# A planned operation order for a gated linear-attention block: a planner that holds GpSimd's small operations back behind VectorE's two-operand operations

## The chip, the cores and the metric

The kernel runs on 1 core of one Trainium2 chip. It is one launch that reads its inputs from HBM and writes its output there. The metric is device microseconds of one execution; lower is better. Before the change the median of three runs is 526.1 us (525.42 to 526.38).

## The reference

The input x has 2048 rows (tokens) of 512 values, all fp32. After a layer norm two branches start from the same normalized rows, and their product is added to x:

```python
x = A_x
xn = _layernorm(x, axis=-1)
s = _A_ref(xn, A_wqkv, A_wo)                        # linear attention
g = _silu(_B_ref(xn, B_w1, B_w2, B_w3, B_w4))       # shift mixer and MLP
return x + s * g
```

The attention has 32 heads of 16 values. With phi(t) = t+1 for t > 0, else exp(t), it forms per head the matrix kv = sum over tokens of phi(k) v and the vector z = sum of phi(k), and for each token o = phi(q) kv / phi(q) z; o is multiplied by wo. It isn't causal, so kv needs all tokens before any o can be made.

```python
h = _gelu(_layernorm(x, axis=-1) @ w1)
# the four 128-column groups of h are shifted by +1, -1, +2, -2 tokens
hs = jnp.concatenate([g0, g1, g2, g3], axis=-1) @ w2
x1 = x + hs
h2 = _gelu(_layernorm(x1, axis=-1) @ w3) @ w4       # 512 -> 1376 -> 512
return x1 + h2
```

## The kernel before, in words

**Tiling.** There are 16 row tiles of 128 tokens, in 4 blocks of 4 tiles (512 tokens). The rows come twice: as they are (x) and with columns on the partitions (xt). Matmuls in fp32 are split: an operand a is rounded to a shorter form, ah (usually on ScalarE, `rounded`, line 451 on), and the rest al = a - ah is made on VectorE (`split`, line 460). A product is three matmuls, ah bh, al bh, ah bl. So names end in h and l. A few matmuls with a column of sums (wqm, w1m, zp) or small weights (kv, m) are done in full fp32, in two passes.

**Stages.** In the first part each tile i gets k (`key`, line 727), q (`query`, 740) and four matmul groups into g (`gram`, 750: the sum of k times x over tokens, in the four accumulators acc); per block, h (`mix1`, 794) and the w2 product by a seven-product scheme on halves (`mix2` and `seven`, 850 and 757; banks pbm, pam, pem). Then from g the matrices kv and m are made, and the second part does w3 and w4 for each block (`up_last`, `up_pair`, `down`; banks pb, pa, pe and acc) and the attention output s (`attend`, `attend_pair`). `gate` (1118) joins both and stores.

**What each tile needs from the small operations.** `moments` (575) takes mean and variance of a tile on VectorE (BN_STATS, BN_AGGREGATE, into mv). `scale_x` (585) makes from them, on GpSimd, w (variance plus eps), rs (its power -1/2, `power`, line 580), ns = -rs and nm = mean times ns, for one, two or three tiles at once. ScalarE uses rs, ns and nm as scales for the relu and exp of k and q (kr, kt, qr, qe) and for x itself. `scale_u` (596) makes pu and au, from which `spread_a` and `join_a` (603, 612) make a row of factors (ab on TensorE, ar on ScalarE, a store to and a load from DRAM: abc) by which h is multiplied (ht). `split_halo` (640) copies the two edge tokens on either side of a block into u_h and u_l, 16 operations of two values per partition on GpSimd for each block. `mixed` (866) makes the second norm's factors rs2 and nm2 per block and the normalized y, which VectorE transposes.

**GpSimd also issues DMAs** that add into their target (`gather`, 217): the sum over phi(k) into zacc, qe onto qr in DRAM (pqd), x onto o, and the three that add the chunks of w1 into w1t (`center`, 554). The next of these waits until the one before has landed. What stands behind such a waiting DMA on GpSimd's queue waits too.

**What sets the order.** No engine order is written by hand. `Plan.add` (96) records each operation with its engine, a planned duration and what it reads and writes. `deadlines` (238) gives every operation a due time, from the nominal time of the TensorE operation that needs it back through its producers (`backward`, 259: a producer is due before its consumer by its latency, a DMA by 4 us and 4 us per MB); an operation that reads PSUM is due at the latest PATIENCE after it can start. `nudged` (232) moves single due times sooner, by 0.25 us times the number in the table SOONER (operation number, number). `emit` (265) then runs a list schedule: for each engine it computes for each ready operation the earliest start, from the engine, the inputs, the buffer slots and, for operations marked `two` (VectorE or GpSimd with large operands in SBUF, line 169 on), the variable `port`; among those that could start within `slack` of the earliest it takes the one with the earliest due time, and emits it. On TensorE, an operation later in the program may go first if it lies within `window` us; `lead` bounds how long before its due time a tile is allocated. The planned times decide only the order in which operations stand on each engine's queue (SP's and GpSimd's queues among them). On the chip each queue runs in that order, and an operation starts as soon as its own semaphores allow.

**Buffers.** counts (424): 89 SBUF pieces of 512 columns, 4 PSUM banks "mm" and 4 "acc". The four h products of a block fill the four mm banks, so the next k needs a bank that ht has freed.

Of the kernel before, what the change touches and what calls it, by code (L numbers as in the profile page):

```python
# [85 lines left out]
class Plan:  # L86
# [6 lines left out]
    def new(self, tag, name, dtype=F32, width=512, rows=P):  # L93
        return Tile(self, tag, name, dtype, width, rows)

    def add(self, eng, busy, lat, reads, writes, emit, two=False, table=None, mb=0.0):
        op = Op()
        op.eng, op.busy, op.lat, op.emit, op.two, op.table, op.mb = eng, busy, lat, emit, two, table, mb
        op.pre, op.post, op.tiles, op.opens = {}, [], {}, False
        op.order = len(self.ops)  # L100
# [56 lines left out]
    def act(self, out, src, func, scale=1.0, bias=None):  # L157
        nc = self.nc
        psum = out.tile.psum or src.tile.psum
        lat = .17 + out.n / 1200 + (.09 if isinstance(scale, View) else 0) + (0 if psum else .02)  # L160
        table = 0 if func == AF.Exp else 1 if func in (AF.Gelu_apprx_tanh, AF.Tanh) else None

        def emit():
            kw = {} if bias is None else {"bias": bias.get()}
            nc.scalar.activation(out.get(), src.get(), func, scale=get(scale), **kw)  # L165

        self.add("ACT", lat - .1, lat, [src, scale, bias], [out], emit, table=table)
# [55 lines left out]


    GAP = .06
    PATIENCE = 3.0
    COLD, COLD_TILL = 1.84, 5.8
    SAFE = 2.0
    early = 0.0
# [8 lines left out]
    def deadlines(self, first):  # L238
# [8 lines left out]
        for op in self.ops:  # L247
# [3 lines left out]
            elif any(t.psum for t in op.tiles):  # L251
                op.due = min(op.due, op.at + self.PATIENCE)
            elif op.soon:
# [5 lines left out]
    def backward(self):  # L259
        for op in reversed(self.ops):  # L260
            if op.eng != "PE":
                for o in op.post:
                    op.due = min(op.due, o.due - self.GAP - (4.0 + op.mb * 4 if op.mb else op.lat))

    def emit(self, first, lead, reserve, window, ahead, table=()):
        self.deadlines(first)
# [10 lines left out]
        free = {e: 0.0 for e in avail}  # L277
        slots = {tag: [(0.0, i) for i in range(n)] for tag, n in self.counts.items()}
        port, dma = 0.0, 0.8
        under = [0.0] * 8, [0.0] * 8  # L280
        table = 0
        done = set()
# [2 lines left out]
        while left:  # L285
# [5 lines left out]
            for e, cands in avail.items():  # L291
                picks = []
                low = INF
                for op in cands:
                    s = max(free[e], op.ready)
                    if op.mb:
                        s = max(s, under[e == "POOL"][0] + self.GAP)
                    if op.two and s < port:
                        s = port
                    if op.table is not None and op.table != table:  # L300
                        s = max(s, free[e] + 1.28)
                    ok = True
                    fresh = [t for t in op.tiles if t.ap is None]
                    for t in fresh:
                        if t.tag not in slots:
                            continue
                        q = slots[t.tag]
                        need = sum(1 for u in fresh if u.tag == t.tag)
                        if len(q) < need:
                            ok = False  # L310
                            break
                        s = max(s, q[need - 1][0] + self.GAP)
                        if e == "PE":
                            if op is not front and (len(q) < 2 or op.nom - front.nom > ahead):
                                ok = False
                                break
                        elif t.tag in lead:
                            n = lead[t.tag] * (1.5 if len(q) > reserve[t.tag] else 1)
                            s = max(s, op.due + slip - n - t.early)
                    if not ok:  # L320
                        continue
                    if e == "PE" and op.nom - front.nom > window:
                        continue
                    q = s
                    if op.table is not None and op.table != table and op.due + slip < s:
                        q = s - 1.28
                    picks.append((q, s, op))
                    low = min(low, q)
                if not picks:
                    continue  # L330
                slack = .02 if e == "PE" else 0.15
                s, op = min(((s, op) for q, s, op in picks if q <= low + slack), key=lambda x: (x[1].due, x[1].order))
                if best is None or s < best[0]:
                    best = (s, op)
            if best is None:
                raise RuntimeError("no operation can go: " + str({t: len(q) for t, q in slots.items()}))
            s, op = best
            e = op.eng
# [19 lines left out]
                under[soft].append(op.end)  # L358
            if op.two:
                port = op.end if e == "POOL" else free[e]  # L360
            if op.table is not None:
                table = op.table
            for t in op.tiles:
# [23 lines left out]
def linear_attn_gated_by_mixer(  # L387
# [43 lines left out]
    pl = Plan(nc, pools, counts, ("acc", "mm"))  # L431
# [813 lines left out]
    b = NQ - 1  # L1245
# [43 lines left out]
    for b in range(NQ):  # L1289
# [50 lines left out]
        else:  # L1340
# [17 lines left out]
                gate(b * QT + QT - 1, a, o, D // 2, late=True, by_dma=False, whole=o > 0)  # L1358

    SOONER = (  # L1360
# [6 lines left out]
    )  # L1367
    pl.emit(first=6.0, lead={"p": 10.0, "w": 10.0, "ab": 10.0}, reserve={"p": 8, "w": 1, "ab": 0}, window=7.0,
            ahead=6.0, table=SOONER)


# [35 lines left out]
```

## Time and profile before

| | before |
|---|---|
| runs, us | 526.38, 526.1, 525.42; median 526.1 |
| profiled execution, us | 525.5 |
| its span, us | 523.3 |
| granted TensorE clock, mean | 0.997 |
| HBM read and written, MB | 60.33 and 30.81 |
| mean DMA rate, GB/s | 191 |

The span goes from the first to the last instruction of the profiled execution; the execution's own time is 2.2 us longer. Engines: PE is TensorE (PEld its weight loads), DVE VectorE, ACT ScalarE, POOL GpSimd, SP the queue that issues most DMAs. A timeline row gives start, duration, engine, line of the kernel, operation, output <- inputs by the program's names (buffer and tile numbers left out), form and count, and in brackets the idle time of that engine just before it, with what ended it. Matmuls are pipelined and their ends are modelled, so two rows overlap; the distance between starts is the safer measure. In a windows row stand the window, its length, the busy time and instructions of PE, PEld, DVE, ACT and POOL, the granted clock, the DMA share and GB/s.

### The profile page before, as it was taken

The numbers are of one execution on the slowest core, as the hardware profiler recorded it, in microseconds if no ns is written. First come the engines' busy times: TensorE is split into PE (matmuls) and PEld (weight loads), VectorE is DVE, ScalarE is ACT, GpSimd is POOL, SyncE is SP. The second block draws the span as 40 slices with busy tenths as digits, with TensorE's granted clock in tenths as the row PEclk, the third lists the DMA queues.
The fourth block names the chain that finished last, engine by engine and source line by source line (L and its number), as shares of the span: only waits on it lengthen the run. The fifth ranks groups of instructions, "written<-read, shape, count | busy, mean of one in ns | idle before, by whom it ended". The sixth has DMA issues, their size and how long they took to land.

```text
span 523.3 us, 8899 instructions
## 1 busy us (share of the span) xinstructions
PE 514.9 (98%) x3027; PEld 448.5 (86%) x3027; DVE 374.3 (72%) x743; ACT 319.4 (61%) x649; POOL 112.1 (21%) x207
## 2 busy tenths in 40 slices
PE   8999999999999999999999999999999999999996
PEld 7777788888888888898899889899899898999985
DVE  5949885658474837999997557897667678396735
ACT  4678995587458847958756655546463366543721
POOL 3374612721273023211200022000040000310000
PEclk9999999999999999999999999999999999999998
DMA  8957849763984369999585759838489376994904
GB/s 240 335 116 180 157 123 235 154 164 94 188 214 142 69 132 200 262 275 307 198 283 176 244 144 220 279 114 231 108 166 314 126 228 129 213 263 153 352 4 121
DMA packets 73713, 100.13 MB, mean 191 GB/s; under 512 B 7892, under 2 KB 31716, under 8 KB 73668
## 3 DMA queue, kind: packets, MB, share of 16 engines
q1 hardware_dynamic: 62436, 79.24, 47.5%
q0 software_dynamic: 11088, 20.19, 23.7%
q8 instruction: 24, 0.39, 0.3%
q14 instruction: 21, 0.17, 0.1%
q10 hardware_dynamic: 144, 0.13, 0.1%
HBM read 60.33 MB, written 30.81 MB: 174 GB/s over the span
## 4 chain that ended last, share of the span: by engine, by line
PE 82%; ACT 6%; DMA 5%; POOL 2%; DVE 2%; issue 1%; SPq 0%; ACTq 0%; POOLq 0%
PE acc L146 22%; PE pb L146 10%; PE h L146 6%; PE g L146 6%; PE q L146 5%; PE pe L146 5%; PE k L146 5%; PE pbm L146 4%; PE pbs L146 3%; DMA w1t<-in_w 3%; PE pa L146 2%; PE a L146 2%; PE pem L146 2%; PE pes L146 2%; PE s L146 2%
## 5 line engine op out<-in xcount | busy, mean ns | idle before, releaser
L221 POOL DMA_DIRECT2D xo<-x1d x12 | 10.7, 1124 | 166.0 <-ACT xo L165 165.9
L221 POOL DMA_DIRECT2D zacc<-kr x16 | 14.4, 899 | 79.1 <-DVE kr L197 71.9
L221 POOL DMA_DIRECT2D th<-in_x x14 | 12.1, 888 | 71.1 <-issue 47.9
L165 ACT ACTIVATE p<-pb 128x256 f32<-128x256 f32 x20 | 7.6, 381 | 30.6 <-PE pb L146 30.3
L197 DVE SCALAR_TENSOR_TENSOR kr<-kt,kr 128x512 f32<-128x512 f32 x16 | 11.1, 691 | 17.0 <-ACT kt L165 17.0
L221 POOL DMA_DIRECT2D o<-x x16 | 15.2, 948 | 34.6 <-DVE o L187 26.1
L165 ACT ACTIVATE gf<-gf 128x512 f32<-128x512 f32 (+1 forms) x40 | 20.9, 523 | 0.9
L197 DVE SCALAR_TENSOR_TENSOR kt<-wneg,mv,k 128x512 f32<-128x512 f32 x16 | 11.9, 743 | 10.9 <-PE k L146 10.8
L165 ACT ACTIVATE x<-x,nm,rs 128x512 f32<-128x512 f32 x16 | 12.1, 806 | 10.5 <-POOL nm L187 10.5
L221 POOL DMA_DIRECT2D pqd<-qe x16 | 17.3, 1079 | 4.6 <-ACT qe L165 3.9
L165 ACT ACTIVATE th<-xo 128x512 f32<-128x512 f32 (+1 forms) x16 | 9.7, 614 | 13.0 <-DVE xo L187 12.1
L165 ACT ACTIVATE p<-pe 128x256 f32<-128x256 f32 x20 | 7.7, 384 | 16.3 <-PE pe L146 16.3
L187 DVE TENSOR_TENSOR gf<-pa,p 128x256 f32<-128x256 f32 x20 | 8.5, 423 | 11.0 <-ACT p L165 5.4
L577 DVE BATCH_NORM_STATS2 st<-o 128x6 f32<-128x512 f32 x16 | 10.9, 686 | 6.5 <-DMA o<-x 6.0
L165 ACT ACTIVATE kr<-kt,rs 128x512 f32<-128x512 f32 x16 | 11.5, 718 | 5.5 <-POOL rs L583 4.2
L187 DVE TENSOR_TENSOR gf<-u,pe 128x256 f32<-128x256 f32 x20 | 8.3, 417 | 7.8 <-PE pe L146 7.8
L165 ACT ACTIVATE qe<-q,ns 128x512 f32<-128x512 f32 x16 | 10.8, 676 | 4.0 <-PE q L146 3.8
L197 DVE SCALAR_TENSOR_TENSOR qz<-pq,zb 128x512 f32<-128x512 f32 x16 | 10.8, 684 | 2.3 <-PE acc L146 2.3
L165 ACT ACTIVATE y<-o,nm,rs 128x512 f32<-128x512 f32 x16 | 11.9, 802 | 0.6 <-POOL nm L192 0.6
L187 DVE TENSOR_TENSOR f_10l<-gf,f_10h 96x512 fp32r<-96x512 f32 x4 | 2.7, 679 | 13.2 <-ACT gf L165 7.5
L192 POOL TENSOR_SCALAR w<-mv 128x4 f32<-128x4 f32 (+3 forms) x11 | 5.5, 498 | 30.9 <-DVE mv L578 30.6
L165 ACT ACTIVATE ht<-ht 128x512 f32<-128x512 f32 x16 | 9.5, 624 | 4.1 <-DVE ht L187 4.0
(1567 smaller groups left out, 2203.2 us busy)
## 6 DMA issues: line engine op xcount, KB each, us to landing
w_s<-in_w SPq DMA_DIRECT2D x28, 256.0 KB, 4.9
x<-in_x SPq DMA_DIRECT2D x16, 256.0 KB, 5.4
zacc<-kr POOLq DMA_DIRECT2D x16, 256.0 KB, 3.4
pqd<-qr SPq DMA_DIRECT2D x16, 256.0 KB, 2.6
pqd<-qe POOLq DMA_DIRECT2D x16, 256.0 KB, 5.0
o<-x POOLq DMA_DIRECT2D x16, 256.0 KB, 4.6
x1d<-o SPq DMA_DIRECT2D x16, 256.0 KB, 4.5
pq<-pqd SPq DMA_DIRECT2D x16, 256.0 KB, 4.7
```

The lines of the kernel that those rows point to most:

```text
L146: lambda: nc.tensor.matmul(out.get(), lhs.get(), rhs.get(), start=start, stop=stop, skip_group_check=more))
L165: nc.scalar.activation(out.get(), src.get(), func, scale=get(scale), **kw)
L187: self.vec(eng, out, [a, b], lambda: self.e(eng).tensor_tensor(out.get(), a.get(), b.get(), op=op), True)
L192: lambda: self.e(eng).tensor_scalar(out.get(), a.get(), get(s1), get(s2), **kw), False,
L197: lambda: self.nc.vector.scalar_tensor_tensor(out.get(), a.get(), get(s), b.get(), op0=op0, op1=op1),
L221: lambda: self.nc.gpsimd.dma_start(out.get(), get(src), accum_op=ALU.add), mb=mb)
L577: pl.add("DVE", .62, .69, [xv], [st], lambda: nc.vector.bn_stats(st.get(), xv.get()))
```

## The change

The same operations are emitted, in another order. The planner's `emit` gets a list, lock, of the last eight planned stretches in which VectorE runs an operation marked `two`; the planned start of a GpSimd operation that is neither a DMA nor marked `two` is moved to 0.02 us after such a stretch when it would fall into it. No wait is added to the program for it. Constants of the planner change with it: an operation that reads PSUM may wait 5 us instead of 3, a DMA is due 1 us earlier, the slack of the choice on all engines but TensorE is 0.4 us instead of 0.15, window is 12 us instead of 7, the lead of tiles "w" 20 us instead of 10; and the table SOONER is another one.

```diff
     GAP = .06
-    PATIENCE = 3.0
+    PATIENCE = 5.0
...
-                    op.due = min(op.due, o.due - self.GAP - (4.0 + op.mb * 4 if op.mb else op.lat))
+                    op.due = min(op.due, o.due - self.GAP - (5.0 + op.mb * 4 if op.mb else op.lat))
...
         port, dma = 0.0, 0.8
+        lock = [(-1.0, -1.0)] * 8
...
                     if op.two and s < port:
                         s = port
+                    if e == "POOL" and not op.mb and not op.two:
+                        s = next((b + .02 for a, b in lock if a <= s < b), s)
...
-                slack = .02 if e == "PE" else 0.15
+                slack = .02 if e == "PE" else 0.4
...
                 port = op.end if e == "POOL" else free[e]
+            if op.two and e == "DVE":
+                lock = lock[1:] + [(s, free[e])]
...
     SOONER = (
-        23, 920, 25, 567, 27, 1578, 32, 434, 33, 142, 37, 71, 40, 69, 41, 8, 43, 71, 47, 73, 49, 1817, 51, 1534,
...
+        23, 795, 26, 123, 28, 878, 29, 115, 31, 67, 32, 4, 34, 76, 35, 9, 37, 23, 38, 8, 41, 19, 44, 14, 47, 13,
...
     )
-    pl.emit(first=6.0, lead={"p": 10.0, "w": 10.0, "ab": 10.0}, reserve={"p": 8, "w": 1, "ab": 0}, window=7.0,
+    pl.emit(first=6.0, lead={"p": 10.0, "w": 20.0, "ab": 10.0}, reserve={"p": 8, "w": 1, "ab": 0}, window=12.0,
             ahead=6.0, table=SOONER)
```

What this does to the queues, from the changed program's instruction order (most differences lie in the first 80 us and from 223 to 262 us of the profile before):

| engine | before | after |
|---|---|---|
| VectorE, start | u_0h, wk_0h, wk_0l, u_0l | u_0h, u_0l, wk_0h, wk_0l |
| TensorE, start | ksum of chunks 0 and 1, then k0 and k1 of chunk 1 | ksum of chunk 0; those of 1, 2 and 3 (h) after chunk 1's k0 and k1 |
| GpSimd | w1t DMA ahead of tile 1's w, rs, ns, nm | behind them |
| GpSimd | second w1t DMA, four halo operations, w, rs, ns, nm of tiles 2 and 3 | second w1t DMA, w, rs, ns, nm of tiles 2 and 3 |
| GpSimd | first pqd DMA, then w, pu, au of block 1 | w, pu, au, then the first pqd DMA |
| SP | loads of w2 among and behind the stores pqd | loads of w1 first, then xt, x and w2, all ahead of the first pqd store |
| TensorE | q3, w1m, gram of tile 3, k4 | q3, gram of tile 3, k4, w1m |
| VectorE | w_s x4, moments of tiles 4, 5, 7, w_0l ... | moments of tiles 4 to 7, two w2 forms, kt4, w_s x4, w_0l ... |
| VectorE | w_t4l, ht0 x4 | ht of group 0, w_t4l, the other three ht |
| TensorE, 245 to 260 us | s0 and s1 (24 matmuls each) spread among the pb, pe products | s0 and s1 behind them, with single acc matmuls between them |
| ScalarE, 250 to 257 us | y12, y13, p1, y14, y15, p5 | y12, y13, y14, a weight copy, y15, p1, two copies, p5 |
| VectorE, 245 to 250 us | m_b and gf operations, then the moments of tiles 13 and 15 | moments first, then m_b and gf |

10 rows, old and new, of the table SOONER are left out of this document.

## The prediction

> **What bounds the kernel now.** I read the page first (busy time and the chain of waits), then TensorE's own timeline row by row, and then, for each hole in it, the timelines of the engines that end it.
>
> ```profile
> span 523.3 us, 8899 instructions
> PE 514.9 (98%) x3027; PEld 448.5 (86%) x3027; DVE 374.3 (72%) x743; ACT 319.4 (61%) x649; POOL 112.1 (21%) x207
> PE 82%; ACT 6%; DMA 5%; POOL 2%; DVE 2%; issue 1%; SPq 0%; ACTq 0%; POOLq 0%
> ```
>
> TensorE is busy for 514.9 of 523.3 us and holds 82% of the chain, so an order of the same operations can win only what TensorE waits. How long it waits is the distance between two matmul starts, less the step at which matmuls follow each other. The chain gives that step: twelve 512-wide matmuls in 2.77 us (0.23 us each), six 256-wide ones in 0.71 us (0.12 us each).
>
> ```profile
> 101.40 2.77 PE k L146 x12
> ...
> 499.95 0.71 PE pes L146 x6
> ```
>
> ```profile
> 34.44 0.50 PE L146 MATMUL g<-k2h,x2h 128*128 128x512 f32 x1
> 35.16 0.50 PE L146 MATMUL g<-k2l,x2h 128*128 128x512 f32 x1 [0.23 <-DVE k2l L197]
> ...
> 40.61 1.02 PE L146 MATMUL w1m<-w1t,ones 128*128 128x512 f32 x2
> ...
> 49.92 0.40 PE L146 MATMUL q<-wq_3h,u_3l 128*128 128x512 f32 x1
> 50.70 0.27 PE L151 MATMUL ab<-ident,au 128*4 128x128 f32 x1 [0.39 <-POOL au L583]
> ...
> 61.72 0.39 PE L146 MATMUL h<-u_3h,w_3l 128*128 128x512 f32 x1
> 62.43 0.51 PE L146 MATMUL k<-wk_0h,u_0h 128*128 128x512 f32 x1 [0.32 <-DVE ht L187]
> ...
> 75.73 0.28 PE L146 MATMUL pem<-w_t1h,hs10l 128*128 128x256 f32 x1
> 76.41 0.39 PE L146 MATMUL pbm<-w_t2h,hs20h 128*128 128x256 f32 x1 [0.40 <-ACT p1m L165]
> ...
> 256.27 0.28 PE L146 MATMUL s<-m_b11h,q1h 128*128 128x256 f32 x1
> 257.14 0.38 PE L146 MATMUL pe<-yb220h,w_s1h 128*128 128x256 f32 x1 [0.59 <-ACT p L165]
> ```
>
> Start to start, less the step, the holes are 35.16-34.44-0.23 = 0.49; 50.70-49.92-0.23 = 0.55; 62.43-61.72-0.23 = 0.48; 75.73 to 76.41 less 0.12 = 0.56; 256.27 to 257.14 less 0.12 = 0.75. The matmul after a hole takes about 0.1 more (its weights were not loaded ahead), and 0.27 more goes just before 34.44. Together: some 3.6 us, all in the first 80 us but one. After 260 us there is no hole worth naming. So the gain has a ceiling near 3.6 us; the loss has none.
>
> **The change, part by part.** It adds and removes no operation: every engine has the same instructions in another order. What counts is what stands ahead of the instruction that ended each hole, in the changed program's order. I go from the start to the end.
>
> First the reason for holding small operations back. The same operation (two values per partition) takes 0.73 us while VectorE works without a gap and 0.20 us when it has stopped:
>
> ```profile
> 28.03 0.73 POOL L648 TENSOR_TENSOR u_0l<-hal,u_0h 128x2 fp32r<-128x2 f32 x1
> ...
> 29.44 0.20 POOL L648 TENSOR_TENSOR u_1l<-hal,u_1h 128x2 fp32r<-128x2 f32 x1
> ```
>
> The planner's start times are no waits, though; a queue starts an operation when its inputs are there. Only places in the queue change.
>
> Start, +0.35 us. VectorE now makes u_0l second, ahead of its half of wk_0h and of wk_0l:
>
> ```profile
> 5.12 0.29 DVE L192 TENSOR_SCALAR u_0h<-xt 128x256 fp32r<-128x256 f32 x1 [5.12 <-DMA xt<-in_xt]
> 5.33 0.28 DVE L192 TENSOR_SCALAR wk_0h<-wk_s 128x256 fp32r<-128x256 f32 x1
> 5.73 0.69 DVE L187 TENSOR_TENSOR wk_0l<-wk_s,wk_0h 128x512 fp32r<-128x512 f32 x1
> 6.34 0.42 DVE L187 TENSOR_TENSOR u_0l<-xt,u_0h 128x256 fp32r<-128x256 f32 x1
> ```
>
> TensorE waits for both wk_0 pieces; they come up to 0.42 later, and the short wait for u_0l goes. Bounds 0 and +0.45. The sum over wk (ksum) now ends before k0 and k1 do, so kt of block 0 starts about as early as VectorE's list did; k0l and x1l stay ahead of their matmuls by some 0.2 us. I take nothing for that stretch.
>
> Hole at 34.4 us, -0.87 (0.27+0.49+0.1). It goes back through kr of tile 2 to GpSimd:
>
> ```profile
> 18.04 1.09 POOL L221 DMA_DIRECT2D w1t<-in_w  x1 [5.75 <-DMA w1t<-in_w]
> ...
> 27.34 0.95 POOL L221 DMA_DIRECT2D w1t<-in_w  x1 [1.39 <-DMA w1t<-in_w]
> ...
> 29.85 0.23 POOL L192 TENSOR_SCALAR w<-mv 128x2 f32<-128x2 f32 x1
> ```
>
> ```profile
> 10.08 0.74 POOL L192 TENSOR_SCALAR w<-mv 128x1 f32<-128x1 f32 x1 [7.01 <-DVE mv L578]
> ...
> 12.10 0.19 POOL L187 TENSOR_TENSOR nm<-mv,ns 128x1 f32<-128x1 f32 x1
> ```
>
> ```profile
> 16.27 0.68 DVE L577 BATCH_NORM_STATS2 st<-x 128x6 f32<-128x512 f32 x1
> ```
>
> The second w1t gather waits until the first has landed, and everything on GpSimd queues behind it. Then came halo operations from 28.03 on, and only at 29.85 the statistics of tiles 2 and 3. In the new order these stand directly behind the gather: 28.03 instead of 29.85, 1.8 us sooner. Against that, the first gather now stands behind the four operations of tile 1's statistics (for tile 0 from 10.08 to 12.29, 2.2 us), and tile 1's moments take about the place that tile 2's had on VectorE, 16.27 to 16.95: the gather starts near 19.1, 1 us later. Left are 0.85 us, and TensorE itself comes 0.35 later: together more than the hole. Bounds -0.87 and +0.15 (first rival).
>
> The gather took 9 us to land. The Trainium skill (DMA: Bandwidth & Descriptors, section Queues, rings and completion order) says that each DMA engine takes turns packet by packet between the queues that have work. By that it would land in far less than 9 us beside the loads, also after a later start, and the next term would be zero; the trace (18.04 to 27.05) shows no such turn, and I go by the trace.
>
> Third gram (tile 3), +0.35. w1m moves from ahead of it to behind k4, so TensorE is there at 40.61+0.35-0.87 = 40.1. ScalarE needs 9.42 us from kr of tile 2 to k3h, and VectorE 1.43 from k3h's start to k3l's end:
>
> ```profile
> 30.92 0.72 ACT L165 ACTIVATE kr<-kt,rs 128x512 f32<-128x512 f32 x1 [3.44 <-POOL rs L583]
> ...
> 40.34 0.71 ACT L165 ACTIVATE k3h<-kr,tiny 128x512 fp32r<-128x512 f32 x1
> ```
>
> With kr at 30.1, k3l ends near 40.9, and its matmul wants it at 40.3: 0.6, less up to 0.3 of ScalarE waits that the new order of x3, kr3, kt3 takes out. Bounds -0.1 and +0.8.
>
> Hole at 50 us, -0.55. The last au waited because the moments of its three tiles stood behind w1's centering on VectorE and ended late:
>
> ```profile
> 46.49 1.87 DVE L577 BATCH_NORM_STATS2 st<-x 128x6 f32<-128x512 f32 x3
> ...
> 48.50 0.66 DVE L187 TENSOR_TENSOR w_0l<-w_s,w_0h 128x512 fp32r<-128x512 f32 x1
> ```
>
> ```profile
> 49.60 1.04 POOL L583 TENSOR_TENSOR au<-pu,nhalf 128x4 f32<-128x4 f32 x1
> ```
>
> Now these moments stand ahead of the centering, and au ahead of the first pqd gather, so it is ready before q4 is through. In exchange the centering starts only after k4: from w1m's end VectorE needs four w_s operations and w_0l, 0.6 each (the three moments above go at 0.62), so about 3.1, and TensorE has 12 x 0.23 of q4, two small transposes and two matmuls of h, about 3.4. That cover is thin: without it, up to 0.3. Bounds -0.55 and 0. The loads of w2 that VectorE now uses ahead of the centering stand on SP's queue ahead of the first pqd store, which waits for qr; so they come before that wait and hold nothing up.
>
> Hole at 62 us, -0.59 (0.48+0.11). k5 needs a PSUM bank, and the first ht, which frees one, stood behind the whole of w2's splitting:
>
> ```profile
> 61.69 2.48 DVE L187 TENSOR_TENSOR ht<-h,abc 128x512 f32<-128x512 f32 x4
> ```
>
> In the new order ht0 goes before w_t4l and fewer w2 operations stand ahead of it, so it has a start of at least one operation (0.6), and more as VectorE runs earlier. Bounds -0.59 and 0.
>
> Hole at 76 us, -0.5. p1m could not be copied before the second table load and two exponentials:
>
> ```profile
> 72.58 1.28 ACT L165 ACT_TABLE_LOAD   x1
> ...
> 75.99 0.36 ACT L165 ACTIVATE p1m<-pbm 128x256 f32<-128x256 f32 x1
> ```
>
> With ht early, gelu and all that follows move ahead by up to 2 us (the last ht waits for h3 on TensorE), TensorE by some 1.3; I count most of 0.67. Bounds -0.67 and 0.
>
> Hole at 256 us, -0.85 (0.75+0.1). Two y copies that waited for GpSimd's nm stood ahead of p5:
>
> ```profile
> 249.61 1.50 POOL L192 TENSOR_SCALAR w<-mv 128x4 f32<-128x4 f32 x1 [10.57 <-DVE mv L578]
> ...
> 253.03 0.55 POOL L192 TENSOR_SCALAR nm<-nm 128x4 f32<-128x4 f32 x1
> ```
>
> ```profile
> 253.62 1.53 ACT L165 ACTIVATE y<-o,nm,rs 128x512 f32<-128x512 f32 x2 [0.57 <-POOL nm L192]
> ```
>
> Now the last moments stand ten VectorE operations sooner (six of about 0.6, four shorter), and I take 2.7 us of it, since other operations moved ahead of them as well. nm is then there at 253.58-2.7 = 250.9 (times of before). But all four y copies (0.75 each) and a weight copy stand ahead of p1: p1 starts at 250.9+3.0+0.6 = 254.5, before TensorE needs it at 255.46. Bounds -0.85 and +3.7 (second rival: 1.9, and 1.8 gained ahead that is lost).
>
> New waits, +0.65. With s0 moved back, only three 0.23 matmuls lie between the third and fourth product in one bank, where 12 lay, and the gf addition between them comes behind an m_b split: 0.25. And VectorE has no room there:
>
> ```profile
> 240.00:260.00 20.00, 19.41 (x151) 18.61 (x150) 18.62 (x39) 16.53 (x38) 3.72 (x4) 1.00 0.71 235
> ```
>
> (TensorE, weight loads, VectorE 18.62 of 20, ScalarE.) For holes that I can't see I add 0.4, somewhat less than one of the size of those above; bounds of the two together 0 and +1.5.
>
> Sum: +0.35-0.87+0.35-0.55-0.59-0.5-0.85+0.65 = -2.0. The profiled execution took 525.5 us (its span is 523.3), so 523.5; the three runs' median, 526.1, is 0.6 above it, so the runs should show 524.1.
>
> **The rivals.** First, less gain: the first gather lands late. It speaks for it that VectorE has no gap from 13 us until its k1l and x1l are done after 29 us, and that the gather landed slowly in just that stretch. The Trainium skill (SBUF — State Buffer, section Who interferes with whom) says that descriptor writing by GpSimd is starved while VectorE holds the shared port in a two-port mode. If the landing waits for VectorE's stretch, which ends about 0.4 later than 29.3, the second gather goes at 29.9 instead of 28.3, kr of tile 2 comes at 31.7 or somewhat before, and the hole at 34.4 grows to 1.0 instead of vanishing: sum -2.0+0.87+0.15 = -1.0, 525.1. Against it: before, the landing was at 27.05, with VectorE still busy.
>
> Second, slower: the last block's statistics don't come sooner. Four operations took GpSimd 4 us there (249.61 to 253.58), and VectorE, at 18.62 of 20 us, may not follow TensorE's lead. By the clock, p5 then comes 5.0 after nm (3.0 and 0.6 as above, p1 itself, two more copies), where it came 3.1 after it (253.62 to just before 257.14, less its own 0.4). If nm stays at 253.6, p5 is 1.9 later than before, and what TensorE gained ahead is lost in that wait: 526.1+1.9 = 528.0. It turns slower from nm later than 251.7 by the clock; my forecast has it near 249 (250.9 less the 1.8 gained ahead). For it: VectorE's load in that window; against it: the moments' place in the queue.
>
> Third, the change doesn't do what it says: GpSimd's operations start whenever their inputs are there, holding back in a plan is no wait, and the other constants only reshuffle work off the path: 526.1. Against it: the order differs at each of the five holes.
>
> **How the numbers follow.** Forecast 0.70; late gather 0.12; slower 0.11; no effect 0.07. The time is the forecast's, 524.1. Its own range is 522.6 to 525.2 (below: the five terms, -3.36, with next to none of the three losses, so -3.5 at most; above: one hole stays and a second new one opens). The range with the rivals is 522.6 to 526.6: it takes in the late gather and no effect, and leaves out most of the slower case and the tails of the forecast. A measurement of this kernel tells no change apart to about 0.2%, 1.05 us. Faster by more: 0.70 and half of the late gather, 0.76; within: the rest of it and no effect, 0.13; slower: 0.11.
>
> **What would show it.** Right: au, kr of tile 2 (near 30 us) and ht0 (before 61 us) early, no hole over 0.3 us at q4, k5, the first pbm and the pe of the second pair; a hole near 0.6 at the third gram; the first ksum about 0.35 later. Wrong: the first w1t gather landing after 29 us; nm of the last block after 251.7 us; holes of half a microsecond at new places between 223 and 262 us; a last matmul not 1 us earlier than before.

## The result and the profile after

The changed kernel takes 524.37 us in the median of 22 runs (523.29 to 526.04), the kernel before 525.77 us in 22 runs beside it (524.76 to 526.38). The ratio is 0.9974, 95% interval 0.9967 to 0.9982: 1.4 us, or 0.26%, faster. The forecast was 524.1, a gain of 2.0 us on the 526.1 of the three runs known then. The profiled execution took 523.38 us (span 521.3), 2.1 us less than that of before; it was one of the fastest of its 22 (their spans go from 521.2 to 524.0), which matters below.

The page of the changed kernel, busy time and chain of waits:

```profile
PE 514.3 (99%) x3027; PEld 447.6 (86%) x3027; DVE 374.5 (72%) x743; ACT 321.9 (62%) x649; POOL 110.2 (21%) x207
...
PE 91%; DMA 4%; ACT 2%; DVE 1%; POOL 1%; SPq 0%; issue 0%; DVEq 0%
```

TensorE's share of the chain went from 82 to 91%. The view of waits for TensorE of the changed kernel (us in total, times, longest) has only two waits left behind the start, both ahead of the gram of tile 3:

```profile
PE warm L146 <- POOL ones L501: 1.1, 1, 1.1
PE k L146 <- DVE wk_0h L192: 0.7, 1, 0.7
PE g L146 <- ACT k3h L165: 0.3, 1, 0.3
PE g L146 <- DVE k3l L197: 0.2, 1, 0.2
```

TensorE's timeline of the changed kernel at the five holes of before, and at the third gram:

```profile
34.39 0.39 PE L146 MATMUL g<-k2h,x2h 128*128 128x512 f32 x1
34.62 0.40 PE L146 MATMUL g<-k2l,x2h 128*128 128x512 f32 x1
...
39.74 0.40 PE L146 MATMUL q<-wq_3h,u_3l 128*128 128x512 f32 x1
40.43 0.50 PE L146 MATMUL g<-k3h,x3h 128*128 128x512 f32 x1 [0.30 <-ACT k3h L165]
41.16 0.51 PE L146 MATMUL g<-k3l,x3h 128*128 128x512 f32 x1 [0.23 <-DVE k3l L197]
...
50.09 0.40 PE L146 MATMUL q<-wq_3h,u_3l 128*128 128x512 f32 x1
50.33 0.27 PE L151 MATMUL ab<-ident,au 128*4 128x128 f32 x1
...
61.36 0.40 PE L146 MATMUL h<-u_3h,w_3l 128*128 128x512 f32 x1
61.59 0.40 PE L146 MATMUL k<-wk_0h,u_0h 128*128 128x512 f32 x1
...
74.75 0.28 PE L146 MATMUL pem<-w_t1h,hs10l 128*128 128x256 f32 x1
74.87 0.28 PE L146 MATMUL pbm<-w_t2h,hs20h 128*128 128x256 f32 x1
...
255.03 0.39 PE L146 MATMUL acc<-w_0h,f_0h 128*128 128x512 f32 x1
255.26 0.28 PE L146 MATMUL pe<-yb220h,w_s1h 128*128 128x256 f32 x1
```

At 34.4, 50, 62, 76 and 256 us the starts now lie one step apart (0.23 or 0.12 us): all five holes are gone. Left is the third gram, where 39.74 to 40.43 and 40.43 to 41.16 are 0.46 and 0.50 us over the step.

The two kernels run the same 3027 matmuls, so the time lost is read by comparing the start of the n-th matmul in both profiles (after less before; the first is number 0):

| stretch (us of before) | foretold | measured | from the difference at its two ends |
|---|---|---|---|
| start, to matmul 60 | +0.35 | 0.00 | 15.97 in both |
| 16 to 33 | 0 | +0.23 | 0.00 to +0.23 |
| hole at 34.4 | -0.87 | -0.88 | +0.23 to -0.65 |
| third gram, with w1m moved behind k4 | +0.35 | +0.81 | -0.63 to +0.18 |
| hole at 50 | -0.55 | -0.55 | +0.18 to -0.37 |
| hole at 62 | -0.59 | -0.59 | -0.36 to -0.95 |
| hole at 76 | -0.5 | -0.67 | -0.97 to -1.64 |
| 83 to 254 (new waits) | +0.65 with the last row | +0.47 | -1.63 to -1.16 |
| hole at 256 | -0.85 | -0.89 | -1.16 to -2.05 |
| 265 to the last matmul | | +0.11 | -2.05 to -1.94 |

The last matmul starts at 516.46 instead of 518.40 us. Within the last row the difference first grew to -2.58 us (near 470 us) and then shrank again; no run here shows what moved this half microsecond either way, so agreement of the sum to a tenth is partly chance.

### The profile page after: what moved, and what is told of

Read it like the earlier page. It is cut to its first block, busy times and chain, and to the rows that moved or that the text cites. A ratio compares the mean times of both kernels' runs of the same rounds, so it can differ in the third digit from the quotient of the medians.

```text
span 521.3 us, 8899 instructions
## 1 busy us (share of the span) xinstructions
PE 514.3 (99%) x3027; PEld 447.6 (86%) x3027; DVE 374.5 (72%) x743; ACT 321.9 (62%) x649; POOL 110.2 (21%) x207
## 4 chain that ended last, share of the span: by engine, by line
PE 91%; DMA 4%; ACT 2%; DVE 1%; POOL 1%; SPq 0%; issue 0%; DVEq 0%
PE acc L146 23%; PE pb L146 11%; PE h L146 9%; PE g L146 7%; PE k L146 6%; PE q L146 6%; PE pe L146 6%; PE pbm L146 4%; PE pbs L146 3%; PE pa L146 3%; PE pem L146 2%; PE s L146 2%; PE a L146 2%; PE pes L146 2%; DMA w1t<-in_w 2%; PE pam L146 1%
## 5 line engine op out<-in xcount | busy, mean ns | idle before, releaser
L221 POOL DMA_DIRECT2D o<-x x16 | 14.1, 878 | 36.8 <-DVE o L187 13.4
L197 DVE SCALAR_TENSOR_TENSOR th<-th,so 128x512 f32<-128x512 f32 (+1 forms) x17 | 11.2, 660 | 3.5 <-ACT th L165 2.4
L192 POOL TENSOR_SCALAR w<-mv 128x4 f32<-128x4 f32 (+3 forms) x11 | 4.3, 393 | 38.8 <-DVE mv L583 38.4
L165 ACT ACTIVATE xo<-acc 128x512 f32<-128x512 f32 x12 | 7.2, 599 | 8.3 <-PE acc L146 7.5
L187 DVE TENSOR_TENSOR ht<-h,abc 128x512 f32<-128x512 f32 x16 | 10.6, 685 | 1.9 <-PE h L146 1.3
```

Of the source, the lines that this page charges most:

```text
L187: self.vec(eng, out, [a, b], lambda: self.e(eng).tensor_tensor(out.get(), a.get(), b.get(), op=op), True)
L192: lambda: self.e(eng).tensor_scalar(out.get(), a.get(), get(s1), get(s2), **kw), False,
L197: lambda: self.nc.vector.scalar_tensor_tensor(out.get(), a.get(), get(s), b.get(), op0=op0, op1=op1),
L221: lambda: self.nc.gpsimd.dma_start(out.get(), get(src), accum_op=ALU.add), mb=mb)
```

## The experiments

Twelve kernels, each timed in turns with the kernel before. Where a queue's order was edited, the planner ran as in the changed kernel, the named operations were moved on their queue, and nothing else was touched.

| kernel | runs | median, us | before beside it | ratio, 95% interval |
|---|---|---|---|---|
| lock_alone | 5 | 530.21 | 525.73 | 1.008 (1.0068 to 1.0093) |
| no_lock | 6 | 524.41 | 525.73 | 0.9966 (0.9953 to 0.9979) |
| first_part | 6 | 528.68 | 525.73 | 1.0057 (1.0044 to 1.0069) |
| first_part2 | 12 | 524.55 | 525.95 | 0.9971 (0.996 to 0.9982) |
| late_part | 11 | 525.21 | 525.73 | 0.9989 (0.998 to 0.9997) |
| g3_alone | 12 | 523.92 | 525.95 | 0.9962 (0.995 to 0.9974) |
| g3_both | 12 | 526.66 | 525.95 | 1.0006 (0.9994 to 1.0018) |
| stats_back | 12 | 526.37 | 525.62 | 1.0011 (1.0001 to 1.002) |
| ht_nm | 4 | 529.35 | 525.62 | 1.0053 (1.0033 to 1.0073) |
| warm_more | 6 | 523.96 | 525.95 | 0.9955 (0.9939 to 0.9972) |
| ones_back | 11 | 523.83 | 525.81 | 0.9969 (0.9959 to 0.9979) |
| combined | 5 | 523.36 | 525.62 | 0.9955 (0.9943 to 0.9967) |

**The lock with the old constants and table, and the new ones without the lock.**

```diff
 lock_alone (to before)
+        lock = [(-1.0, -1.0)] * 8
...
+                    if e == "POOL" and not op.mb and not op.two:
+                        s = next((b + .02 for a, b in lock if a <= s < b), s)
...
+            if op.two and e == "DVE":
+                lock = lock[1:] + [(s, free[e])]
```

no_lock takes the same five lines out of the changed kernel.

> The kernel before with the lock list alone; its constants and its table SOONER stay. Theory (the table is fitted to one plan: the due times it moves close the holes of that plan and no other, so a planner whose starts shift needs a new table): slower than before by 1 to 4 us, 526.8 to 529.8, with holes of half a microsecond at places where before had none. Rival (holding GpSimd's small operations back in the plan is what gains): 524.4 or less, as the changed kernel, with the holes at 34.4, 50, 62, 76 and 256 us gone or halved.

> The changed kernel without the lock list; its constants and its table stay. TensorE's order keeps all but a handful of its places, GpSimd's differs in some twenty. Theory (the gain is in the places of a few operations at five holes, which constants and table set; the lock moves mainly halo operations that nobody waits for): 524.0 to 525.0, within 0.6 us of the changed kernel, and the five holes stay closed. Rival (the lock carries the gain): 525.5 or more, with at least two of the holes back.

The lock alone is 4.5 us slower than before, a little more than the upper end foretold. Its waits of TensorE, same view as above:

```profile
PE q L146 <- DVE wq_0l L187: 0.7, 1, 0.7
PE pb L146 <- DVE gf L187: 0.7, 2, 0.5
PE pb L146 <- ACT p L165: 0.7, 1, 0.7
PE pbm L146 <- ACT p1m L165: 0.6, 1, 0.6
```

The wait for p1m is an old one, grown; those for wq_0l and gf are new, and the third is the hole of 256 us on another bank. TensorE's last matmul starts 4.1 us later than before. Without the lock the changed kernel is as fast as with it (524.41 against 524.37 us), and in its profile none of the five holes is there. So what names the change did not make it faster: the gain is in which operations the constants and the table bring forward at a few places. Which of the two does it is open, since no run takes the constants and the table apart. A table found for one plan lost 4.5 us on another (lock_alone) and nothing on a third (no_lock).

**Half of the order at a time.** Up to 150 us of the plan every queue follows one kernel's order, behind it the other's.

```diff
-every queue: the changed kernel's order
+first_part, first_part2: the changed kernel's up to 150 us, before's behind it
+late_part: before's up to 150 us, the changed kernel's behind it
```

> On every queue the changed kernel's order for what is planned before 150 us, and the order of before for the rest. Theory (each hole is local, TensorE is never made up or slowed behind it): TensorE 1.3 to 1.6 us ahead of before at 150 us of the profile and still so at the end, the hole at the pe of the second pair near 256 us still there (0.7 to 1 us): time 524.1 to 524.7. Rival (the stretch from 223 to 262 us is bound by VectorE, so TensorE's earlier arrival only waits longer there): the hole at 256 us grows to 1.5 us or more and the time is 525.3 to 525.9.

> On every queue the order of before for what is planned before 150 us, and the changed kernel's for the rest. Theory (the last block's factors come sooner because of their moments' place on VectorE): the four holes of the first 80 us as before, none over 0.3 us between 240 and 262 us, nm of the last block near 249 us: 0.6 to 0.9 us less than before, 524.9 to 525.2. Rival (the late order needs TensorE's earlier arrival, or gives back behind 262 us what it wins): 525.6 to 526.3.

> first_part again, with the same order on every queue, but a buffer that comes free earliest in the plan is taken first, as the planner does it, instead of the one released first. Theory (first_part lost its time to a buffer whose store had not landed, near 405 us, and to nothing else; up to there TensorE was 1.2 us ahead): no hole over 0.5 us behind 262 us, the one at 256 us still there, time 524.3 to 524.9. Rival (before's order behind 150 us does not stand an earlier TensorE): a wait of 1 us or more behind 262 us again, time above 525.5.

first_part missed both of its expectations. TensorE was 1.2 us ahead of before at 390 us, then waited 3.1 us near 405 us for VectorE, and VectorE had stood 1.38 us before f_1l, whose buffer still waited for a store. VectorE's timeline of first_part:

```profile
401.35 0.69 DVE L187 TENSOR_TENSOR f_1l<-gf,f_1h 128x512 fp32r<-128x512 f32 x1 [1.38 <-DMA out<-th]
```

The queues' order didn't ask for that; it came from the buffers, which this kernel handed out in the order of their release. With the planner's rule (first_part2, order unchanged) the loss is gone and the first half alone brings 1.4 us (525.95 to 524.55). (Its profile began slowly: matmul 60 started 1.73 us later than in before's profile, and the last matmul at the same time.) The hole near 256 us stands in it as before:

```profile
255.88 0.28 PE L146 MATMUL s<-m_b11h,q1h 128*128 128x256 f32 x1
256.74 0.39 PE L146 MATMUL pe<-yb220h,w_s1h 128*128 128x256 f32 x1 [0.59 <-ACT p L165]
```

The second half alone brings 0.5 us, at the upper edge of the times foretold, without that hole. So, as far as the intervals tell, the halves are independent and the holes local. That the two gains add up to more than the whole (1.4 and 0.5 against 1.4) lies within the intervals.

**GpSimd's order behind the second w1t DMA.**

```diff
 stats_back, GpSimd
-w rs ns nm (tiles 2, 3), pu, au, u_1l, u_2h, u_2l, u_3h, u_3l
+pu, au, u_1l, u_2h, u_2l, u_3h, w rs ns nm (tiles 2, 3), u_3l
```

> The changed kernel with GpSimd's w, rs, ns, nm of tiles 2 and 3 moved back behind the four halo operations that follow, as in before; nothing else moves. Theory (kr of tile 2 comes 1.0 to 1.6 us later after the landing of the gather; ScalarE works without a gap from there to k3h, so k3h is as much later, and VectorE's u, w_s and w_0l with it): a wait of 0.4 to 1.0 us ahead of the second gram matmul of tile 2 is back, the wait at tile 3's gram stays, and the kernel is 0.6 to 1.3 us slower than the changed one, 525.0 to 525.7. Rival (TensorE waits at tile 3's gram in any case, so what comes back at tile 2 is saved at tile 3): within 0.2 us of the changed kernel, 524.2 to 524.6.

Its median is 2.0 us above the changed kernel's, more than foretold: pu and au now also stand ahead of w (in before they stood behind nm), which makes the step from the second DMA's issue to kr of tile 2 4.35 us instead of 2.37. ScalarE's timeline of stats_back:

```profile
33.33 0.73 ACT L165 ACTIVATE kr<-kt,rs 128x512 f32<-128x512 f32 x1 [4.94 <-POOL rs L627]
...
42.59 0.73 ACT L165 ACTIVATE k3h<-kr,tiny 128x512 fp32r<-128x512 f32 x1
```

and of the changed kernel:

```profile
30.38 0.72 ACT L165 ACTIVATE kr<-kt,rs 128x512 f32<-128x512 f32 x1 [3.81 <-POOL rs L588]
...
39.65 0.73 ACT L165 ACTIVATE k3h<-kr,tiny 128x512 fp32r<-128x512 f32 x1
```

From kr to k3h it is 9.26 us in the one and 9.27 in the other: ScalarE hands a delay on one to one. The rival (saved again at tile 3) falls: this profile began slowly, with TensorE 1.84 us later than in the changed kernel's at matmul 60; behind the gram of tile 2 it was 2.9 us later, and behind that of tile 3 as well.

**The third gram.**

```diff
 g3_alone, ScalarE
-qe0 qr0 qe1 qr1 x3 kr3 x3h kt3 qe2 qr2 k3h
+qe0 qr0 x3 kr3 x3h kt3 qe1 qr1 k3h qe2 qr2
 g3_both, besides: VectorE
-w_f w_f w_b11l kt4 w_s x4 w_0l w_1l w_2l w_3l
+kt4 w_s x4 w_0l w_1l w_2l w_f w_f w_b11l w_3l
 ScalarE
-w_t1h w_t2h w_b22h ar0 w_3h w_0h w_2h w_1h ar1
+w_b22h ar0 w_3h w_0h w_2h w_1h w_t1h w_t2h ar1
```

> The changed kernel with ScalarE's qe and qr of tile 1 moved behind kt of tile 3, and those of tile 2 behind k3h; nothing else moves. k3h then starts about 1.1 us sooner and the wait ahead of tile 3's gram (0.46 and 0.50 us in the changed kernel) goes. Theory (behind the gram VectorE and ScalarE set the pace: u's splits wait for ScalarE, then the w2 forms and w_s, so w_0l does not come sooner): the time won comes back as a wait of 0.6 to 0.9 us between the gram of tile 3 and the first matmuls of h, and the kernel is 0 to 0.4 us faster than the changed one, 524.0 to 524.4. Rival (the hole was the only limit there): TensorE keeps 0.9 to 1.1 us, 523.3 to 523.5.

> The same moves, and the two forms of w2, the split of w_b11l (VectorE) and the roundings w_t1h, w_t2h (ScalarE) moved behind the splitting of w1, so that the centering of w1 starts some 1.3 us sooner. Theory: now the 0.9 to 1.1 us are kept, and the time is 523.3 to 523.6, faster than the changed kernel. Rival (VectorE, busy over 90% from 40 to 60 us, hands the delay on to w2's last forms, the first ht or the first pbm): 524.2 to 525, with a hole of 0.5 us or more between 58 and 78 us.

In g3_alone k3h comes 8.12 us behind kr instead of 9.27, as foretold. ScalarE's timeline:

```profile
32.51 0.72 ACT L165 ACTIVATE kr<-kt,rs 128x512 f32<-128x512 f32 x1 [3.81 <-POOL rs L627]
...
40.63 0.72 ACT L165 ACTIVATE k3h<-kr,tiny 128x512 fp32r<-128x512 f32 x1
```

No matmul of the third gram waits, but this profile alone doesn't show that the moves did it: TensorE came there 2.1 us later than in the changed kernel's profile, from a slow start, and no_lock, which came as late without the moves, doesn't wait there either. g3_both and warm_more (below) do: both bring TensorE there 0.3 us late, and with the moves the wait is gone, without them it is 0.45 and 0.50 us. TensorE's timeline of g3_alone shows where a wait came up, which no_lock doesn't have:

```profile
52.76 0.50 PE L146 MATMUL h<-u_0h,w_0l 128*128 128x512 f32 x1 [0.39 <-DVE w_0l L187]
```

It is 0.55 us over the step there, and the median is 0.45 us below the changed kernel's, with intervals that overlap. g3_both made more of that wait instead of less: w_3l stood behind the w2 forms (VectorE did it at 53.22 us), TensorE waited 1.4 us for it, ScalarE stood 1.96 us ahead of w_t1h with ar and the next q behind it, and the hole at 76 us was back with 0.45. The rival's place was wrong too (52 us, not 58 to 78), but its cause was right in this profile: VectorE handed the delay on. The profile (525.01 us) is the shortest of the twelve runs. Three lie near 525.1 and nine between 526.3 and 526.9, above the times of both expectations, and what costs those nine a further 1.5 us isn't seen.

**ht, and the last block's moments.**

```diff
 ht_nm, VectorE
-ht (group 0), w_t4l
+w_t4l, ht (group 0)
...
-moments of tile 15, m_b11l ... f_10l
+m_b11l ... f_10l, moments of tile 15
```

> The changed kernel with two moves on VectorE, 190 us apart and read each at its own place. First, ht of group 0 behind w_t4l, as in before. Theory A (the place ahead of w_t4l closed the hole at 62 us): k5 waits 0.4 to 0.6 us again. Theory B (ht waited for abc in the changed kernel, which w_t4l can fill; the hole was closed by the earlier au and the shorter queue): k5 waits under 0.2 us. Second, the last tile's moments behind f_10l, some nine VectorE operations later, so that nm of the last block comes 4 to 5.5 us later, near 252.5 us. Theory (all four y copies and one more now stand ahead of p1): p1 2.5 to 3.5 us later, and TensorE waits 2.0 to 2.8 us at the pe of the second pair or just before it: time 526.4 to 527.2. Rival (the y copies do not bound TensorE there): no hole over 0.5 us, 524.2 to 524.8.

The first move cost nothing: k5 shows no wait over 0.1 us. ht waits for abc in either order. VectorE's timeline of ht_nm, and the same place in the changed kernel:

```profile
62.19 2.48 DVE L187 TENSOR_TENSOR ht<-h,abc 128x512 f32<-128x512 f32 x4 [0.62 <-DMA abc<-arow]
```

```profile
60.08 0.69 DVE L187 TENSOR_TENSOR ht<-h,abc 128x512 f32<-128x512 f32 x1 [0.58 <-DMA abc<-arow]
```

So theory B holds: the hole at 62 us closed because abc and VectorE's queue are earlier, not by ht's place ahead of w_t4l. The median is 5.0 us above the changed kernel's, twice what was foretold for the second move. Three of the four runs took 529.2 to 529.5 us at a mean granted clock of 0.994 or 0.995; the fourth, at 1.000, took 526.66, inside the range foretold. In the profile, one of the three, nm ended at 254.81 us, 7.2 later than in the changed profile. TensorE came to this place 1.42 us later than in the changed profile, and left it 6.20 us later: 0.77 for w_al, which the moved moments pushed back on VectorE, 2.12 for p1, and 1.89 more behind that wait. TensorE's timeline and the view of windows (PE, PEld, DVE, ACT, POOL busy, then the granted clock) show the last part:

```profile
254.48 0.39 PE L146 MATMUL pb<-yb110h,w_al 128*128 128x256 f32 x1 [0.51 <-DVE w_al L187]
258.62 0.38 PE L146 MATMUL pb<-yt20h,w_s0h 128*128 128x256 f32 x1 [1.95 <-ACT p L165]
...
260.68 0.41 PE L146 MATMUL pe<-yb220h,w_s1l 128*128 128x256 f32 x1
260.89 0.41 PE L146 MATMUL pe<-yb220h,w_s1h 128*128 128x256 f32 x1
```

```profile
258.60:262.60 4.00, 3.93 (x19) 3.67 (x19) 3.04 (x6) 4.00 (x10) 0.00 (x0) 0.61 0.34 127
```

The 256-wide matmuls go every 0.21 us there instead of every 0.12, at a granted clock of 0.61. So the wait has about the price foretold, and the half rate behind it, which the fourth run seems not to have had, is the rest.

**The start.**

```diff
 warm_more
         pl.mm(warm.cols(n % NC * P, (n % NC + 1) * P), ones.all, ones.all, True, True, slow=True)
+    once = pl.ops[-1].emit
+    pl.ops[-1].emit = lambda: [once() for _ in range(3)]
```

```diff
 ones_back, GpSimd
-memset ones, tiny, zacc
+memset tiny, zacc, ones
```

combined has the longer warming, the four moves of g3_alone, and w_b11l behind w_b21l on VectorE.

> The changed kernel with two more of the warming matmuls ahead of the first k (four more passes of 0.1 to 0.2 us). Theory (the changed kernel's warming starts and ends half a microsecond sooner, since the memset of ones moved ahead on GpSimd; in executions in which the first loads are late TensorE then idles over 1 us and its next matmuls go at 0.43 instead of 0.23 us, which costs up to 2 us there): the median is 0.3 to 0.8 us below the changed kernel's, 523.6 to 524.1, its slowest runs below 525. Rival (the spread comes from the loads alone): 524.3 to 524.8, with the same spread of some 2.5 us.

> The changed kernel with GpSimd's memset of ones back behind that of zacc, as in before; nothing else moves. The first warming matmul then starts near 1.58 us instead of 1.08. Theory (the earlier warming leaves TensorE idle for about a microsecond ahead of the first k, and in five of eight profiles with that start its next matmuls went at half rate until 9 to 10 us): the idle time ahead of the first k is 0.2 to 0.9 us, the matmuls are at 0.23 us from 7.5 us on, the 60th matmul starts near 16.5 us or sooner, and the median is 523.7 to 524.2 with no run above 525. Rival (the memset's place does not matter; the loads do): 524.3 to 524.8 with a spread of over 2 us, and half rate until 9 us or later.

> The changed kernel with the longer warming of warm_more, the four moves of g3_alone on ScalarE, and w_b11l behind w_b21l on VectorE, where VectorE had 0.4 us of room, so that the centering of w1 and w_0l come 0.6 us sooner. Theory (the three waits are separate: the start's, the one at tile 3's gram, and the one of 0.55 us at the first matmul with w_0l that g3_alone put in its place): 523.0 to 523.5, which is 0.9 to 1.4 us below the changed kernel, with no hole over 0.3 us between 34 and 62 us. Rival (as in g3_both, VectorE hands the delay on): a hole of 0.5 us or more between 52 and 78 us, 523.8 or more.

The changed kernel's start in two executions: TensorE's timeline of the changed kernel's profile, and of no_lock's, whose first queues are the same:

```profile
5.57 0.70 PE L146 MATMUL k<-wk_0h,u_0h 128*128 128x512 f32 x2 [0.69 <-DVE wk_0h L192]
...
6.84 0.39 PE L146 MATMUL k<-wk_0l,u_0h 128*128 128x512 f32 x1
7.08 0.40 PE L146 MATMUL k<-wk_0h,u_0l 128*128 128x512 f32 x1
```

```profile
6.42 1.19 PE L146 MATMUL k<-wk_0h,u_0h 128*128 128x512 f32 x2 [1.13 <-ACT wk_1h L165]
...
7.84 0.63 PE L146 MATMUL k<-wk_0h,u_0l 128*128 128x512 f32 x1
8.27 0.63 PE L146 MATMUL k<-wk_0l,u_0h 128*128 128x512 f32 x1
```

In the second the loads came later and the matmuls then went every 0.43 us, until 10.4 us. Of the eight profiles with the changed kernel's start, five reach such a half rate; their matmul 60 (the first is number 0, as in the table) starts at 17.70 to 18.19 us, in the other three at 15.97 to 16.39. The idle time of TensorE ahead of the first k does not tell them apart: it was 0.84 to 1.61 us in the five and 0.69, 1.03 and 1.47 us in the three. In three profiles with the start of before (before, late_part, lock_alone) it starts at 15.97 to 16.47, with the longer warming (warm_more, combined; matmul 64 there) at 16.29 and 16.52, and in ones_back at 15.96. In these six TensorE idled 0.27 us or less ahead of the first k. The nine profiles other than those five reach the 0.23 step by 7.7 us.

warm_more's median is 0.4 below the changed kernel's and its six runs lie within 1.1 us (523.11 to 524.21), the changed kernel's 22 within 2.75. ones_back has the median foretold, 523.83, but two of its eleven runs above 525, which its theory excluded, so the memset's place is at most a part of it. The intervals of both overlap the changed kernel's, so what the longer warming and the memset's place bring isn't settled; that the half-rate start occurs, and how much it takes (about 2 us at matmul 60), is shown.

combined is the fastest kernel here, 523.36 us, 1.0 below the changed one and 2.3 below before; the intervals of its ratio and of the changed kernel's just touch (0.9967). Behind the start its TensorE waits nowhere between 34 and 62 us; the third gram, for instance:

```profile
40.30 0.39 PE L146 MATMUL q<-wq_3h,u_3l 128*128 128x512 f32 x1
40.52 0.39 PE L146 MATMUL g<-k3h,x3h 128*128 128x512 f32 x1
40.75 0.40 PE L146 MATMUL g<-k3l,x3h 128*128 128x512 f32 x1
```

## Why the prediction was right, and where it was not

**Direction and size.** The five holes closed, each by about the term it had, and the sum came out for the profiled execution (-1.94 at the last matmul against -2.0). The median gained 1.4. Two terms were mis-sized and one mechanism was missed; in the profiled execution they cancelled, which is luck. The time, 524.1 against 524.37, came closer than the gain, because the three runs that it started from have a median 0.33 us above that of all 22.

**Start, +0.35: mis-sized.** The sum took VectorE's order for the price. In the profiled execution it was 0.00, since the first loads let VectorE begin 0.66 us sooner (u_0h at 4.46 instead of 5.12 us); in five of the eight profiles with this start it was about 2 us by matmul 60. What was left out is in the same queues: GpSimd's memset of ones moved ahead of zacc's, so the warming starts at 1.08 instead of 1.58 us and is over before the first k has its inputs. That this idle time brings the half rate is likely, not shown: three profiles have it without the half rate. A part of what is lost there comes back at the third gram: in first_part2 and ht_nm TensorE arrives there late and waits 0.34 and 0.38 us instead of 0.96. This fits a median that gained less than the profile; how many of the 22 runs began so was not seen.

**16 to 33 us, nothing: +0.23.** q of tile 0 goes through chunk 1 first now, and wq_1l comes just then on VectorE:

```profile
23.14 0.68 DVE L187 TENSOR_TENSOR wq_1l<-wq_s,wq_1h 128x512 fp32r<-128x512 f32 x1
```

It ends at 23.82, and its matmul starts at 23.87, 0.1 late; two or three such steps make the 0.23.

**Hole at 34.4, -0.87: right, by its own steps.** GpSimd's timeline after:

```profile
18.93 1.09 POOL L221 DMA_DIRECT2D w1t<-in_w  x1
...
28.01 0.87 POOL L221 DMA_DIRECT2D w1t<-in_w  x1 [3.62 <-DMA w1t<-in_w]
28.95 0.29 POOL L192 TENSOR_SCALAR w<-mv 128x2 f32<-128x2 f32 x1
```

The first w1t DMA starts at 18.93 (19.1 foretold) and lands at 27.7, 8.8 us later (9.0 before). kr of tile 2 starts at 30.38 (30.1 foretold), 0.54 sooner than before. With TensorE 0.23 later that is 0.77, just the 0.27+0.49 of the hole, and not the 1.2 that the prediction had. The first rival needed a landing behind 29 us, when VectorE's stretch ends (29.8 here); the landing came 0.7 us later than before, as the DMA's issue came 0.9 later.

**Third gram, +0.35: mis-sized, +0.81, the upper end of its bounds.** The step that failed is the size of the wait for k3h and k3l, which the prediction put at 0.6 less up to 0.3. It was 0.46+0.50 = 0.96 us. kr of tile 2 came 0.28 later than foretold (30.38 against 30.1), TensorE 0.1 earlier (40.0 against 40.1), and ScalarE needed 9.27 us from kr to k3h (9.42 foretold), so the new order of x3, kr3 and kt3 won only half of the 0.3. In before, w1m stood ahead of this gram and hid most of the same wait: its two passes take 0.85 us (measured in the changed kernel, from w1m at 46.58 to the next matmul at 47.43), so of the 1.22 us from 40.61 to 41.83 only about 0.14 was waiting. 0.96 less 0.14 is the 0.81, within 0.01.

**Holes at 50, 62, 76: right in size.** au is ready at 47.85, TensorE wants it at 50.33; the thin cover of the centering held. For the hole at 62 the reason was wrong in part: of the two given, ht_nm shows the second (VectorE's queue and abc are earlier) to suffice.

**Hole at 256, -0.85: right, with more room than foretold.** GpSimd and ScalarE in the changed profile:

```profile
245.00 0.58 POOL L192 TENSOR_SCALAR w<-mv 128x4 f32<-128x4 f32 x1 [7.24 <-DVE mv L583]
...
247.09 0.55 POOL L192 TENSOR_SCALAR nm<-nm 128x4 f32<-128x4 f32 x1
```

```profile
249.82 2.22 ACT L165 ACTIVATE y<-o,nm,rs 128x512 f32<-128x512 f32 x3
...
253.17 0.36 ACT L165 ACTIVATE p<-pb 128x256 f32<-128x256 f32 x1
...
254.51 0.39 ACT L165 ACTIVATE p<-pe 128x256 f32<-128x256 f32 x1
```

nm ends at 247.64 instead of near 249; the y copies don't wait for it any more. The four small operations took 2.6 us instead of 4.0. The slower rival's mechanism is real, as ht_nm shows, but its price left out the half rate that can follow such a wait, 1.89 us in ht_nm's profile.

**New waits, +0.65: right in sum (+0.58),** 0.19 of it between 244 and 254 us, where the fourth product follows the third, the rest in small steps.

**No effect** falls with the result. What it said of holding back is nearly true, though: the lock itself did nothing that could be measured.

## What to carry to other kernels

When a planner's rule, its constants and its table change together, the name of the change says little: take the rule out alone before crediting it. A tuned table can lose more than the change wins when the plan under it moves, so measure it again. A wait that an edit lays bare may have been filled by the operation that the edit moved: price both. Of the queues that feed the first matmuls count everything, a memset too.

## What the hardware showed that was not expected

After a wait of 2.1 us (ht_nm) and of 3.1 us (first_part), TensorE's matmuls ran at half their rate for 3.5 and 3.1 us, with a granted clock of 0.61 and 0.58 in the 4 us windows around those stretches; after one of 1.4 us in g3_both's profile they did not (clock 1.00 from 54 to 58 us). The Trainium skill (TensorE: Matmul & The Clock Gate, section Part 1: The HAM clock gate (the "warmup" mystery)) says that the clock is halved after at least one idle window of about 3.4 us and comes back after a busy one, and that the window runs freely. The half rate and its length agree; 2.1 us of waiting were enough in ht_nm's profile, though one of its four runs kept a mean clock of 1.000.

At the start the same half rate (0.43 us for 512 columns) does not show in the granted clock of the profile. The windows of no_lock from 6.4 to 10.4 us give 1.00:

```profile
6.40:10.40 4.00, 3.98 (x9) 3.08 (x10) 3.97 (x9) 1.69 (x4) 0.00 (x0) 1.00 0.96 300
```

The nine matmuls begun or running in these 4 us say otherwise: at 0.23 us each there would be 17. There the distance between starts is the measure, not the clock column.

The prediction's pair of rows (0.73 us beside a busy VectorE, 0.20 us beside an idle one) is not the whole rule for GpSimd's small operations. In the profile before, the same kind of operation took 0.20 us while VectorE ran a BN_STATS (19.71 to 20.40 us), and 0.53 us at 24.83 us, while VectorE split wq_2 with both operands in SBUF. GpSimd's timeline:

```profile
19.83 0.20 POOL L648 TENSOR_TENSOR u_1l<-hal,u_1h 128x2 fp32r<-128x2 f32 x1
```

So what VectorE runs matters, not only that it runs; no run here changes that alone.
